# An expert layer in seven products a step: gathers asked tile by tile, weight sums spread over the step, another product order, a last step by tiles

## The chip, the cores and the metric

The kernel runs on one core of a Trainium2 chip. The metric is device time of one execution in microseconds, the median of several runs; lower is better. Beside the timed runs there is one profiled execution, whose trace all views here come from.

## The reference

The input x has shape (4, 8, 768, 32). A state-space block (Mamba-2 in chunks) makes y of the same shape; y is laid out as 3072 tokens of 256 numbers, and each token goes through the one expert that its id names:

```python
expert_idx = token_ids * np.int64(2654435761) % np.int64(E)      # E = 8
for e in range(E):
    mask = expert_idx == e
    xe = x[mask]                        # tokens of expert e, D = 256
    h = np.maximum(xe @ w1[e], 0.0)     # F = 1024
    out[mask] = h @ w2[e]
```

All is float32.

## The kernel before

**Two parts.** The first part (to about 85 us) computes the state-space block, stores the tokens' rows to a buffer in HBM (`y_tokens`), and works out from the ids a slot for every token. The change doesn't touch it, but for one constant of the slots. The second part runs the experts.

**Slots and tiles.** The experts are sorted by their number of tokens. Place p has two halves (j = 0, 1) of `HALF[p]` slots each, 202 down to 184; `base[p, j]` is where a half begins among 25 tiles of 128 slots. A tile k is fetched with `gather(k)` (line 477: an indirect DMA on POOL's queue, into one of 8 buffers `xg`), turned with `turn_x(k)` (line 485: two transposes on TensorE into PSUM bank `BT`, one copy by ACT into `xT`), and, when both products of all its slots are done, written out with `put(k, bank)` (line 836: two transposes into bank `BQ`, a copy by ACT into one of 4 buffers `o_sb`, and an indirect DMA on POOL's queue that scatters its rows). `ask(n)` issues the next n gathers.

**Seven products.** Each of an expert's two matrix products is cut into 2 x 2 blocks and done with seven block products instead of eight, after sums of the operands' blocks and before sums of the results, in Winograd's order of sums. `up(p, q0, what, bank, st)` (line 750) does product `what` (1 to 7) of the first matrix product for half of the rows (q0 = 0 or 2): two matmuls, and what DVE or ACT then does with the PSUM bank. `down` (line 801) does a product of the second, in four matmuls. The operands' sums are DVE's: `sums_x` (four sums over an expert's tokens), `sums_h` (four over its hidden tile, one in each of the slots 0 to 3), `sums_w1` and `sums_w2` (four each over an expert's weights, 128 x 512 elements).

Products 6, 7 and 4 of one half share a PSUM bank and add up in it; so do 5 and 3. After 6, DVE evicts `u2` = bank + p1; after 7, `u3` = bank + p1 (line 789); and 7's block also takes z, the bank of product 5, as `hx` = z + u3 (line 791), which ACT then puts through a ReLU. Product 4 may enter the bank only when `u3` has been read out, product 3 only when z has. In `down` it is the same with one bank each (lines 822 to 834).

**The order.** A manual schedule is on: the instructions of an engine run in the order in which the code writes them, and an engine waits at the one whose operands or buffers aren't ready, with all that stands behind it. `step(p)` writes the up products of expert p among the down products of expert p - 1, in seven slots. A slot holds up to two up products, one turn, one put and one down product. In slot 0 the four w1 sums for expert p + 1 follow, in slot 1 the four w2 sums for expert p; from slot 2 on, each slot asks for one gather; slot 4 has `sums_x(p + 1)`. At the end of a step the weights are loaded: two halves of w1 for p + 3, w2 for p + 1, on SyncE's queue. For p = 1, 2 the up products 1 and 2 have been done ahead (`UP_E` has five products), from p = 3 on all seven are in the step (`UP`). `step(E)` has the last expert's down products alone, and the last four puts follow it, then a loop for tokens beyond the slots, which has no rounds with this input.

## Time and profile before

| | |
|---|---|
| runs | 284.52, 287.68, 287.95 us; median 287.68 |
| profiled execution | 285.23 us, its span in the trace 283.4 us |
| busy share of the span | PE 79%, PEld 73%, DVE 71%, ACT 27%, POOL 28% |
| mean granted clock of TensorE | 0.92 |
| indirect DMAs | 25 gathers and 25 scatters, POOL's queue |
| from HBM, to HBM | 26.47 MB, 6.42 MB |

PE stands for TensorE's matmuls and PEld for its weight loads, which overlap them; each matmul in float32 appears as two instructions of the trace. A share over the whole span mixes the two parts, so the expert part is better read in stretches of time, one for each step: its rows give the busy time of each engine there. A row of the timeline has its start and length, and in brackets the idle time of its engine ahead of it, with what ended that.

### The profile page before, as it was taken

The page shows a single profiled execution, that of the slowest core. Times are in us where ns is not written, and L with a number is a line of the kernel's source. Part 1 is how long each engine was busy: PE and PEld are TensorE (multiplying, and loading weights), DVE is VectorE, ACT ScalarE, POOL GpSimd, SP SyncE. Part 2 cuts the span into 40 slices and gives each one's busy share as a digit, 9 for nine tenths or more (in the row PEclk, how much of TensorE's full clock was granted, in tenths as well). Part 3 has the DMA queues.
Part 4 walks back from the last instruction along what each step waited for, and adds up shares of the span by engine and source line. Part 5 has one row for each costly group of instructions (what it writes and reads, how often), then busy time and mean ns, then how long its engine had stood idle before and what let it go on. Part 6 is the DMA issues. An engine that isn't in the chain of part 4 may idle for free. (4 is left out here: it accounts for less than half of the span.)

```text
span 283.4 us, 6377 instructions
## 1 busy us (share of the span) xinstructions
PE 224.9 (79%) x2577; PEld 205.7 (73%) x2579; DVE 201.5 (71%) x393; ACT 76.3 (27%) x177; POOL 79.0 (28%) x113
## 2 busy tenths in 40 slices
PE   7885775576579768798799989499989999999820
PEld 2773654465469758788689989399979999998810
DVE  7879768999808529977977958836876886776310
ACT  4314152043116512210312223221242242313010
POOL 8800003019443760001121501710132130312250
PEclk9689799579958997999999999989999999999995
DMA  5899998507958334015316305610901500500110
GB/s 127 135 173 141 173 178 176 192 22 207 294 173 245 97 106 148 19 21 191 123 57 208 126 2 185 203 38 5 312 20 58 166 26 13 172 33 6 51 59 1
DMA packets 51890, 33.19 MB, mean 117 GB/s; under 512 B 30714, under 2 KB 46194, under 8 KB 51860
## 3 DMA queue, kind: packets, MB, share of 16 engines
q1 hardware_dynamic: 47444, 24.41, 34.4%
q0 software_dynamic: 2400, 6.43, 7.0%
q10 hardware_dynamic: 2016, 1.93, 2.3%
q8 instruction: 21, 0.34, 0.6%
q14 instruction: 9, 0.07, 0.1%
HBM read 26.47 MB, written 6.42 MB: 116 GB/s over the span
## 5 line engine op out<-in xcount | busy, mean ns | idle before, releaser
L847 POOL DMA_INDIRECT out_dram<-o_sb,idx_out x25 | 27.9, 1117 | 73.7 <-ACT o_sb L843 58.9
L480 POOL DMA_INDIRECT xg<-y_tokens,idx_in x25 | 27.5, 1098 | 75.3 <-PE ps L838 46.6
L770 PE MATMUL ps<-t,s 128*128 128x202 f32 (+7 forms) x192 | 37.6, 333 | 2.2 <-DVE t L730 1.6
L770 PEld LDWEIGHTS ps<-t,s 128*128 128x128 f32 x192 | 32.8, 194 | 3.2 <-ACT xT L494 1.8
L812 PE MATMUL ps<-t,s 128*128 128x202 f32 (+7 forms) x192 | 34.9, 326 | 0.0
L812 PEld LDWEIGHTS ps<-t,s 128*128 128x128 f32 x192 | 31.3, 190 | 0.0
L770 PE MATMUL ps<-xT,w 128*128 128x202 f32 (+7 forms) x128 | 26.2, 342 | 0.0
L792 ACT ACTIVATE hx<-hx 128x404 f32<-128x404 f32 (+7 forms) x16 | 8.4, 525 | 57.6 <-DVE hx L791 57.6
L770 PEld LDWEIGHTS ps<-xT,w 128*128 128x128 f32 x128 | 22.6, 200 | 0.8 <-ACT p1e L777 0.7
L572 PE MATMUL ps<-x,w 128*64 128x64 f32 x384 | 15.6, 251 | 7.1 <-issue 2.6
L572 PEld LDWEIGHTS ps<-x,w 128*64 128x64 f32 x384 | 14.7, 164 | 8.3 <-issue 4.5
L770 PE MATMUL ps<-t,w 128*128 128x202 f32 (+7 forms) x64 | 14.5, 351 | 7.1 <-DVE u L789 5.6
L528 DVE COPY_PREDICATED w<-cmask,ps 128x2048 f32<-128x2048 int32 x6 | 15.2, 2532 | 4.9 <-PE ps L523 4.9
L770 PEld LDWEIGHTS ps<-t,w 128*128 128x128 f32 x64 | 11.0, 198 | 9.1 <-DVE u L789 7.3
L838 PE MATMUL ps<-ident,xT 128*128 128x128 f32 x50 | 9.8, 281 | 6.7 <-ACT o_sb L843 6.1
L812 PE MATMUL ps<-hx,s 128*128 128x202 f32 (+7 forms) x64 | 12.1, 331 | 2.5 <-DVE xT L830 2.5
L770 PE MATMUL ps<-xT,s 128*128 128x202 f32 (+7 forms) x64 | 13.8, 344 | 0.0
L843 ACT ACTIVATE o_sb<-ps 128x256 f32<-128x256 f32 x23 | 8.7, 380 | 18.6 <-PE ps L838 12.2
L411 POOL TENSOR_SCALAR laneoh<-iota,lane 128x128 bf16<-128x128 f32 x12 | 9.0, 765 | 16.6 <-DVE stile L400 16.6
L494 ACT ACTIVATE xT<-ps 128x256 f32<-128x256 f32 x23 | 8.6, 377 | 16.6 <-PE ps L488 14.7
L523 PE MATMUL ps<-ce,bt 32*64 32x128 f32 x384 | 8.9, 315 | 5.1 <-ACT ce L251 2.8
L812 PEld LDWEIGHTS ps<-hx,s 128*128 128x128 f32 x64 | 10.5, 189 | 3.4 <-DVE xT L830 3.4
(189 smaller groups left out, 442.1 us busy)
## 6 DMA issues: line engine op xcount, KB each, us to landing
w<-in_moe_w_dram SPq DMA_DIRECT2D x8, 1024.0 KB, 6.4
w<-in_moe_w_dram SPq DMA_DIRECT2D x13, 512.0 KB, 4.8
x<-in_x_dram SPq DMA_DIRECT2D x12, 256.0 KB, 6.4
y_tokens<-y_sb SPq DMA_DIRECT2D x6, 512.0 KB, 3.4
w<-in_moe_w_dram ACTq DMA_DIRECT2D x3, 512.0 KB
raw<-in_B_dram SPq DMA_DIRECT2D x8, 128.0 KB, 6.0
raw<-in_C_dram SPq DMA_DIRECT2D x8, 128.0 KB, 4.7
raw<-in_B_dram SPq DMA_DIRECT2D x8, 64.0 KB, 2.1
```

The lines of the kernel that those rows point to most:

```text
L411: eng.tensor_scalar(out=laneoh[:, i], in0=iota_n, scalar1=lane[:, i:i + 1], scalar2=None, op0=OP.is_equal)
L480: pool_e.indirect_dma_start(out=xg[k], out_offset=None, in_=y_dram[0:n, :], in_offset=bass.IndirectOffsetOnAxis(ap=idx_in[:, k:k + 1], axi ...
L494: act.activation(o, i, AF.Copy)
L523: pe.matmul(out=ps[u * T:(u + 1) * T, BM + b, g * P:(g + 1) * P].rearrange("q (e i) -> q e i", e=2), lhsT=bts[k][r, g, c], rhs=ces[k][r, g ...
L528: dve.copy_predicated(out=m_sb, mask=cmask.bitcast(I32).rearrange("q j i -> q (j i)").unsqueeze(1).to_broadcast([P, NB, 2 * G * T]), data= ...
L572: pe.matmul(out=o[:, 0], lhsT=m_sb[:, b, h * T:(h + 1) * T], rhs=xs[k][:, b * H + h], start=first, stop=True, skip_group_check=True)
L770: pe.matmul(out=ps[:, bank, i * n:(i + 1) * n], lhsT=lhs[:, (q0 + i) * P:(q0 + i + 1) * P], rhs=rhs, start=(first and i == 0), stop=True, ...
L792: act.activation(hq(2), hq(2), AF.Relu)
L812: pe.matmul(out=ps[:, bank, 0:n], lhsT=lhs(q), rhs=rhs(q), start=(first and q == 0), stop=True, skip_group_check=True)
L838: pe.transpose(out=ps[:, bank, i * P:(i + 1) * P], in_=xT[:, i, k * P:(k + 1) * P], identity=ident)
L843: act.activation(o_sb, ps[:, bank, 0:DM], AF.Copy)
L847: st = pool_e.indirect_dma_start(out=out[:], out_offset=bass.IndirectOffsetOnAxis(ap=idx, axis=0), in_=o_sb, in_offset=None, bounds_check= ...
```

## The change

It has four parts.

1. *Gathers.* `ask(1)` moves from "each slot from 2 on" to right behind each `turn_x`. In POOL's queue, before (gathers write `xg`, scatters `out_dram`):

```order
L480 DMA xg<-y_tokens,idx_in 128x256 x23
L847 DMA out_dram<-o_sb,idx_out 3072x256
L480 DMA xg<-y_tokens,idx_in 128x256 x2
L847 DMA out_dram<-o_sb,idx_out 3072x256 x24
L953 TENSOR_LOAD nov_i
```

and now:

```order
L482 DMA xg<-y_tokens,idx_in 128x256 x19
L859 DMA out_dram<-o_sb,idx_out 3072x256
L482 DMA xg<-y_tokens,idx_in 128x256 x3
L859 DMA out_dram<-o_sb,idx_out 3072x256
L482 DMA xg<-y_tokens,idx_in 128x256
L859 DMA out_dram<-o_sb,idx_out 3072x256
L482 DMA xg<-y_tokens,idx_in 128x256
L859 DMA out_dram<-o_sb,idx_out 3072x256 x2
L482 DMA xg<-y_tokens,idx_in 128x256
L859 DMA out_dram<-o_sb,idx_out 3072x256 x20
L988 TENSOR_LOAD nov_i
```

The 25 gathers and 25 scatters stay; the last six gathers now stand among the scatters, each behind the turn of the tile whose buffer it takes, and 19 instead of 23 come ahead of the first scatter.

2. *Weight sums.* `sums_w1` and `sums_w2` become generators. Each slot takes one sum from each that has been started; w1's starts in slot 0 as before, w2's in slot 3 instead of 1.

3. *Order of products.* `down` has 1, 2, 6, 7, 5, 4, 3 instead of 1, 2, 6, 5, 7, 3, 4; in steps 1 and 2 the up products of both halves are interleaved (`UPS`), the second half's 6, 7 and 4 in bank 0. Whichever of 5 and 7 comes later makes `hx` = z + u3.

Parts 2 and 3 on DVE's queue at the start of step 1, before (`t` are the sums over the hidden tile and over tokens, `s` the weight sums, `u` and `hx` evictions of up products):

```order
L741 SCALAR_TENSOR_TENSOR t_1625<-hx,h_1496 128x808
L786 TENSOR_TENSOR u_1630<-ps,p1e 128x2x200
L711 TENSOR_TENSOR s_1643<-w_1224 128x512
L712 TENSOR_TENSOR s_1643<-s_1643,w_1224 128x512
L713 TENSOR_TENSOR s_1643<-w_1224 128x512
L714 TENSOR_TENSOR s_1643<-w_1224,s_1643 128x512
L744 TENSOR_TENSOR t_1625<-hx,t_1625 128x808
L789 TENSOR_TENSOR u_1651<-ps,p1e 128x2x200
L791 TENSOR_TENSOR hx<-ps,u_1651 128x2x200
```

and now:

```order
L741 SCALAR_TENSOR_TENSOR t_1621<-hx,h_1496 128x808
L786 TENSOR_TENSOR u_1626<-ps,p1e 128x2x200
L713 TENSOR_TENSOR s_1643<-w_1224 128x512
L744 TENSOR_TENSOR t_1621<-hx,t_1621 128x808
L789 TENSOR_TENSOR u_1648<-ps,p1e 128x2x200
L798 TENSOR_TENSOR hx<-ps,u_1648 128x2x200
L786 TENSOR_TENSOR u_1654<-ps,p1e 128x2x200
L713 TENSOR_TENSOR s_1643<-s_1643,w_1224 128x512
L746 SCALAR_TENSOR_TENSOR t_1621<-hx 128x808
L795 TENSOR_TENSOR hx<-ps,p1e 128x2x200
L793 TENSOR_TENSOR hx<-ps,u_1626 128x2x200
```

Between the first eviction `u` (product 6) and the second (product 7) stood four weight sums and one over the hidden tile; now there are one and one, and the four w2 sums that stood behind `hx` have gone from this place.

4. *The last step by tiles.* The last half of the last expert begins at a tile's start (48 slots ahead of it stay empty; there are 25 tiles as before). The step of the last down products is written out: order 1, 2, 6, 7, 4, 5, then the puts of the two tiles that need no product 3, then product 3 in two pieces of 128 and 56 columns, each with its eviction and its put, the copies by ACT and DVE in turn; a put now follows its slot's product. Behind the last put of the expert before, POOL gets a `drain()`, an instruction that waits until the engine has nothing left to do (the listing of the order leaves it out). TensorE's queue in the last step, before (`xT` are transposes for puts):

```order
L838 MATMUL ps<-ident,xT 128x128 x2
L812 MATMUL ps<-h_2525,w_2470 128x184 x4
L838 MATMUL ps<-ident,xT 128x128 x2
L812 MATMUL ps<-hx,w_2470 128x184 x4
L838 MATMUL ps<-ident,xT 128x128 x2
L812 MATMUL ps<-t_2595,s_2517 128x184 x12
L812 MATMUL ps<-hx,s_2517 128x184 x4
L812 MATMUL ps<-t_2595,w_2470 128x184 x4
L838 MATMUL ps<-ident,xT 128x128 x8
```

and now, from its second product on:

```order
L821 MATMUL ps<-hx,w_2470 128x184 x4
L850 MATMUL ps<-ident,xT 128x128 x2
L821 MATMUL ps<-t_2595,s_2553 128x184 x4
L850 MATMUL ps<-ident,xT 128x128 x2
L821 MATMUL ps<-t_2595,s_2553 128x184 x4
L821 MATMUL ps<-t_2595,w_2470 128x184 x4
L821 MATMUL ps<-t_2595,s_2553 128x184 x4
L850 MATMUL ps<-ident,xT 128x128 x4
L814 MATMUL ps<-hx,s_2553 128x128 x4
L850 MATMUL ps<-ident,xT 128x128 x2
L814 MATMUL ps<-hx,s_2553 128x56 x4
L850 MATMUL ps<-ident,xT 56x128 x2
```

All eight transposes stood behind the last product; now four stand ahead of product 3 and two behind each of its pieces.

The diff, cut to its core:

```diff
@@ slots
     for pj in order:
+        if pj == order[-1]:
+            at = -(-at // P) * P
         base[pj] = at
@@ weight sums
+    def sums_w(w, s, q):
+        q = [q(i // 2, i % 2) for i in range(4)]
+        for i, (x0, x1, op) in enumerate(((q[2], q[3], OP.add), (s[:, 0], q[0], OP.subtract),
+                                          (q[2], q[0], OP.subtract), (q[1], s[:, 1], OP.subtract))):
+            yield dve.tensor_tensor(out=s[:, i], in0=x0, in1=x1, op=op)
@@ up
         elif what == 7:
-            u3 = work("u3", 2)
-            dve.tensor_tensor(out=u3, in0=src, in1=st["p1"], op=OP.add)
-            z = ps[:, st["z"], 0:2 * n].rearrange("q (i n) -> q i n", i=2)
-            dve.tensor_tensor(out=hq(2), in0=z, in1=u3, op=OP.add)
-            act.activation(hq(2), hq(2), AF.Relu)
+            st["u3"] = work("u3", 2)
+            dve.tensor_tensor(out=st["u3"], in0=src, in1=st["p1"], op=OP.add)
...
+        if what in (5, 7) and "z" in st and "u3" in st:
+            dve.tensor_tensor(out=hq(2), in0=st["z"], in1=st["u3"], op=OP.add)
+            act.activation(hq(2), hq(2), AF.Relu)
@@ down
+        if parts:
+            for i, (c0, c1) in enumerate(parts):
+                for q in range(Q4):
+                    pe.matmul(out=ps[:, bank, c0:c1], lhsT=lhs(q), rhs=rhs(q)[:, c0:c1], start=False, stop=True,
+                              skip_group_check=True)
+                dve.tensor_tensor(out=xT[:, 0, slots(p, 1)][:, c0:c1], in0=ps[:, bank, c0:c1], in1=st["u2"][:, c0:c1],
+                                  op=OP.add)
+                put(slots(p, 1).start // P + i, (BQ, BT)[i], (act, dve)[i], c1 - c0)
+            return
@@ step
-    DOWN = [1, 2, 6, 5, 7, 3, 4]
+    UPS = [(0, 6, 1), (0, 5, 2), (0, 7, 1), (2, 6, 0), (0, 4, 1), (0, 3, 2), (2, 7, 0), (2, 5, 2), (2, 4, 0), (2, 3, 2)]
+    DOWN = [1, 2, 6, 7, 5, 4, 3]
...
                 turn_x(k)
                 turned.add(k)
+                ask(1)
...
             if s == 0 and 0 < p < E - 1:
-                sums_w1(p + 1, dve)
-            if s == 1 and 0 < p < E:
-                sums_w2(p, dve)
-            if s >= 2:
-                ask(1)
+                sums.append(sums_w1(p + 1))
+            if s == 3 and p > 0:
+                sums.append(sums_w2(p))
+            for x in sums:
+                next(x, None)
@@ the last step
-    for p in range(E + 1):
+    for p in range(E):
         step(p)
-    last = [k for k in outs if done_at[k] == E - 1]
-    for i, k in enumerate(last):
-        put(k, (BQ, BT, 0, 1)[i % 4], (act, dve)[i % 2])
+    dst = {}
+    puts = [k for k in outs if done_at[k] == E - 2]
+    for s, w in enumerate([1, 2, 6, 7, 4, 5]):
+        if s < 4:
+            sums_h(E - 1, s)
+        down(E - 1, w, 3 + BK[w], dst)
+        if puts:
+            put(puts.pop(0), BQ)
+            if not puts:
+                pool_e.drain()
...
+    mid = [k for k in outs if done_at[k] == E - 1 and k * P < base[E - 1, 1]]
+    for i, k in enumerate(mid):
+        put(k, (BQ, BT)[i % 2], (act, dve)[i % 2])
+    down(E - 1, 3, 3 + BK[3], dst, PARTS)
```

More of the change, by code (lines that the diff above doesn't have):

```diff
@@ L705, in slots, with sums_w1, sums_w2 @@
         return slice(base[p, j], base[p, j] + HALF[p])
-    def sums_w1(p, eng):
-        w = w1s[p]
-        q = lambda i, k: w[:, k, i * FH:(i + 1) * FH]
-        s = s1[p] = spool.tile([P, 4, FH], F32, name="s1")
-        eng.tensor_tensor(out=s[:, 0], in0=q(1, 0), in1=q(1, 1), op=OP.add)
-        eng.tensor_tensor(out=s[:, 1], in0=s[:, 0], in1=q(0, 0), op=OP.subtract)
-        eng.tensor_tensor(out=s[:, 2], in0=q(1, 0), in1=q(0, 0), op=OP.subtract)
-        eng.tensor_tensor(out=s[:, 3], in0=q(0, 1), in1=s[:, 1], op=OP.subtract)
-    def sums_w2(p, eng):
-        w = w2s[p]
-        q = lambda i, k: w[:, k * Q4:(k + 1) * Q4, i * P:(i + 1) * P]
-        s = s2[p] = spool.tile([P, 4, Q4, P], F32, name="s2")
-        eng.tensor_tensor(out=s[:, 0], in0=q(1, 0), in1=q(1, 1), op=OP.add)
-        eng.tensor_tensor(out=s[:, 1], in0=s[:, 0], in1=q(0, 0), op=OP.subtract)
-        eng.tensor_tensor(out=s[:, 2], in0=q(1, 0), in1=q(0, 0), op=OP.subtract)
-        eng.tensor_tensor(out=s[:, 3], in0=q(0, 1), in1=s[:, 1], op=OP.subtract)
+    def sums_w(w, s, q):
[3 more added lines that the diff above has]
+            yield dve.tensor_tensor(out=s[:, i], in0=x0, in1=x1, op=op)
+    def sums_w1(p):
+        w = w1s[p]
+        s1[p] = spool.tile([P, 4, FH], F32, name="s1")
+        return sums_w(w, s1[p], lambda i, k: w[:, k, i * FH:(i + 1) * FH])
+    def sums_w2(p):
+        w = w2s[p]
+        s2[p] = spool.tile([P, 4, Q4, P], F32, name="s2")
+        return sums_w(w, s2[p], lambda i, k: w[:, k * Q4:(k + 1) * Q4, i * P:(i + 1) * P])
     def sums_x(p):
@@ L799, in up, with down @@
             act.activation(hq(1), hq(1), AF.Relu)
-    def down(p, what, bank, st):
+        if what in (5, 7) and "z" in st and "u3" in st:
+            dve.tensor_tensor(out=hq(2), in0=st["z"], in1=st["u3"], op=OP.add)
+            act.activation(hq(2), hq(2), AF.Relu)
+    def down(p, what, bank, st, parts=()):
         n = HALF[p]
@@ L826, in down @@
             st["z"] = bank
+            if "u3" in st:
+                dve.tensor_tensor(out=o(1, 1), in0=src, in1=st["u3"], op=OP.add)
         elif what == 7:
-            u3 = work("du3")
+            u3 = st["u3"] = work("du3")
             dve.tensor_tensor(out=u3, in0=src, in1=st["p1"], op=OP.add)
-            dve.tensor_tensor(out=o(1, 1), in0=ps[:, st["z"], 0:n], in1=u3, op=OP.add)
+            if "z" in st:
+                dve.tensor_tensor(out=o(1, 1), in0=ps[:, st["z"], 0:n], in1=u3, op=OP.add)
         elif what == 3:
@@ L834, in down, with put @@
             dve.tensor_tensor(out=o(1, 0), in0=src, in1=st["p1"], op=OP.add)
-    def put(k, bank, eng=None):
+    def put(k, bank, eng=None, n=P):
         for i in range(DP):
-            pe.transpose(out=ps[:, bank, i * P:(i + 1) * P], in_=xT[:, i, k * P:(k + 1) * P], identity=ident)
+            pe.transpose(out=ps[0:n, bank, i * P:(i + 1) * P], in_=xT[:, i, k * P:k * P + n], identity=ident)
         o_sb = mwork.tile([P, DM], F32, name="o_sb", bufs=4)
         if eng is dve:
-            dve.tensor_copy(out=o_sb, in_=ps[:, bank, 0:DM])
+            dve.tensor_copy(out=o_sb[0:n], in_=ps[0:n, bank, 0:DM])
         else:
-            act.activation(o_sb, ps[:, bank, 0:DM], AF.Copy)
-        scatter(o_sb, idx_out[:, k:k + 1])
+            act.activation(o_sb[0:n], ps[0:n, bank, 0:DM], AF.Copy)
+        scatter(o_sb[0:n], idx_out[0:n, k:k + 1])
     def scatter(o_sb, idx):
@@ L880 @@
                 up(p, q0, what, (2 * p + 4 + q0 // 2) % 8, sts[p, q0])
-    sums_w1(1, dve)
-    sums_w2(0, dve)
+    list(sums_w1(1))
+    list(sums_w2(0))
     for i, k in enumerate(turn_due(0)):
@@ L890 @@
     UP_E = [6, 5, 7, 4, 3]
-    DOWN = [1, 2, 6, 5, 7, 3, 4]
+    UPS = [(0, 6, 1), (0, 5, 2), (0, 7, 1), (2, 6, 0), (0, 4, 1), (0, 3, 2), (2, 7, 0), (2, 5, 2), (2, 4, 0), (2, 3, 2)]
+    DOWN = [1, 2, 6, 7, 5, 4, 3]
     BK = {1: 0, 2: 0, 6: 1, 7: 1, 4: 1, 5: 2, 3: 2}
     outs = sorted(range(NK), key=lambda k: (done_at[k], k))
+    n1 = HALF[E - 1]
+    PARTS = [(c, min(c + P, n1)) for c in range(0, n1, P)]
+    assert base[E - 1, 1] % P == 0 and len(PARTS) == 2
     def step(p):
@@ L902, in step @@
             else:
-                ups = [(q0, w, BK[w]) for q0 in (0, 2) for w in (UP_E if p < NEAR - 1 else UP)]
+                ups = UPS if p < NEAR - 1 else [(q0, w, BK[w]) for q0 in (0, 2) for w in UP]
+        ups = list(ups)
+        sums = []
         downs = list(DOWN) if p > 0 else []
```

6 lines of the change are left out of this document (4 added, 2 removed).

## The prediction

> **What bounds the kernel now.** I first cut the expert part of the trace into its steps. Each row below is one stretch: start and end, its length, then the busy time of PE, PEld, DVE, ACT and POOL, the granted TensorE clock, and DMA. The first seven rows are steps 1 to 7, the eighth is the last step up to the end of the last scatter's issue, the ninth is what follows it.
>
> ```profile
> 110.13:131.42 21.29, 18.18 (x100) 17.22 (x100) 17.45 (x32) 3.50 (x8) 1.02 (x1) 0.96 0.29 96
> 131.42:152.18 20.76, 17.86 (x106) 16.86 (x106) 16.84 (x31) 4.12 (x10) 3.94 (x3) 1.00 0.37 119
> 152.18:173.51 21.33, 20.58 (x128) 19.77 (x127) 16.56 (x31) 6.43 (x17) 4.81 (x4) 1.00 0.26 82
> 173.51:198.85 25.34, 21.33 (x124) 20.75 (x124) 16.66 (x31) 5.95 (x15) 8.05 (x7) 0.93 0.36 118
> 198.85:220.47 21.62, 20.31 (x129) 19.45 (x129) 16.39 (x31) 6.74 (x18) 5.20 (x5) 1.00 0.36 125
> 220.47:239.98 19.51, 19.51 (x126) 18.91 (x125) 16.20 (x31) 5.94 (x16) 3.38 (x3) 1.00 0.24 75
> 239.98:258.36 18.38, 18.38 (x120) 18.14 (x119) 12.76 (x23) 5.15 (x13) 3.44 (x3) 1.00 0.24 80
> 258.36:276.38 18.02, 11.40 (x72) 10.05 (x69) 6.43 (x13) 2.45 (x7) 7.46 (x7) 0.98 0.13 45
> 276.38:283.40 7.02, 0.00 (x0) 0.00 (x0) 0.00 (x0) 0.00 (x0) 0.01 (x1) 0.50 0.01 1
> ```
>
> Steps 6 and 7 are TensorE without a hole. Step 4 does the same products as step 6 on a few more columns and is 5.8 us longer. Steps 1 and 2 have four products fewer and are still longer than step 6. So TensorE bounds the expert part wherever it isn't held up, and the change can win only its holes, plus the 25 us after 258.36. I then read the timeline of TensorE's weight loads and kept the rows with a wait (in brackets: idle time, and what ended it). Two grouped rows of the waits, for 152 to 258.3 us, stand for the small ones.
>
> ```profile
> 116.45 0.64 PEld L770 LDWEIGHTS ps<-t,w 128*128 128x128 f32 x4 [2.06 <-DVE u L789]
> 121.99 1.31 PEld L770 LDWEIGHTS ps<-t,s 128*128 128x128 f32 x8 [0.81 <-DVE hx L796]
> 128.57 1.33 PEld L812 LDWEIGHTS ps<-hx,s 128*128 128x128 f32 x8 [1.17 <-DVE xT L830]
> 137.33 0.63 PEld L770 LDWEIGHTS ps<-t,w 128*128 128x128 f32 x4 [2.25 <-DVE u L789]
> 142.85 1.30 PEld L770 LDWEIGHTS ps<-t,s 128*128 128x128 f32 x8 [0.40 <-DVE hx L796]
> 149.36 1.31 PEld L812 LDWEIGHTS ps<-hx,s 128*128 128x128 f32 x8 [1.17 <-DVE xT L830]
> 163.83 0.20 PEld L838 LDWEIGHTS ps<-ident,xT 128*128 128x128 f32 x2 [1.05 <-ACT o_sb L843]
> 182.21 0.20 PEld L838 LDWEIGHTS ps<-ident,xT 128*128 128x128 f32 x2 [4.25 <-ACT o_sb L843]
> 210.82 0.20 PEld L838 LDWEIGHTS ps<-ident,xT 128*128 128x128 f32 x2 [1.60 <-ACT o_sb L843]
> ...
> PEld ps L770 <- DVE u L789: 0.8, 4, 0.2
> PEld ps L488 <- ACT xT L494: 0.8, 3, 0.3
> ```
>
> The waits of steps 1 and 2 sum to 4.04 and 3.82 us; all six are for a DVE eviction that frees a PSUM bank.
>
> **Gathers behind the tile that frees their buffer.** What held TensorE at 182.21 is on the other queues (POOL, then ACT):
>
> ```profile
> 175.45 0.99 POOL L480 DMA_INDIRECT xg<-y_tokens,idx_in  x1 [13.82 <-PE ps L838]
> 176.75 1.09 POOL L847 DMA_INDIRECT out_dram<-o_sb,idx_out  x1 [0.30 <-issue]
> ...
> 181.78 0.38 ACT L843 ACTIVATE o_sb<-ps 128x256 f32<-128x256 f32 x1 [6.18 <-DMA out_dram<-o_sb,idx_out]
> ```
>
> The last gather stood 13.82 us at the head of POOL's queue, until the transposes of its buffer's tile; the scatters behind it started only then. With four output buffers the fifth copy of ACT waited for the scatter issued at 176.75, and TensorE for the copy. In the changed order a gather stands behind the turn that frees its buffer, so it waits for a transpose just done. The number of gathers and scatters stays. Each is still asked eight tiles, over two steps, ahead of its use. The hole cost more than its length:
>
> ```profile
> 184.26 1.47 PE L770 MATMUL ps<-xT,w 128*128 128x190 f32 x4
> 188.97 0.81 PE L770 MATMUL ps<-xT,w 128*128 128x190 f32 x4
> ...
> 182.20:186.80 4.60, 4.58 (x19) 4.48 (x20) 2.28 (x4) 1.96 (x6) 2.53 (x3) 0.63 0.24 85
> ```
>
> The same four instructions took 1.47 us at 184.26 and 0.81 at 188.97. With a granted clock of 0.63 over 4.60 us, 0.37 x 4.60 = 1.7 us went to slow clock. So step 4 loses 4.25 + 1.7. The Trainium skill (TensorE: Matmul & The Clock Gate, Part 1) says that an idle window of about 3.4 us halves the clock and as long a busy one restores it. The row agrees; by that rule, too, the slow stretch goes with its hole, and the sum stays.
>
> **Weight sums spread, products reordered.** The pitch on DVE comes from neighbours without idle time:
>
> ```profile
> 201.57 0.69 DVE L712 TENSOR_TENSOR s<-s,w 128x512 f32<-128x512 f32 x1
> 202.18 0.68 DVE L713 TENSOR_TENSOR s<-w 128x512 f32<-128x512 f32 x1
> ...
> 114.92 0.99 DVE L744 TENSOR_TENSOR t<-hx,t 128x808 f32<-128x808 f32 x1
> 115.83 0.57 DVE L789 TENSOR_TENSOR u<-ps,p1e 128x400 f32<-128x400 f32 x1
> ...
> 112.49 1.54 PE L812 MATMUL ps<-h,w 128*128 128x202 f32 x8
> 113.87 0.84 PE L770 MATMUL ps<-t,s 128*128 128x200 f32 x4
> ```
>
> A weight sum takes 0.61 us of the queue, a sum over the hidden tile 0.91, an eviction with its dependent one 0.6. A down product takes 1.38 us of TensorE, an up product about 0.68. In step 1 four weight sums (2.4 us) stood ahead of the eviction of product 7, and product 4 followed 7 at once in the same bank: 2.06. Now one sum stands ahead, and 0.68 + 1.38 = 2.06 us of other work lies between 7 and 4. For 121.99, the sums of w2 leave the place ahead of the eviction. For 128.57, product 3 of down no longer follows the read of its bank: product 4, 1.38 us, lies between, against one eviction (0.37) and some 0.27 for a product's end to reach DVE (1.54 less 1.38, the rest of it an estimate). Without waits step 1 is five slots of 2 x 0.68 + 1.38 and two of 1.38, 16.5 us, with 0.04 x 21.29 of slow clock 17.3 (that clock comes from step 0, which is left as it was). I walked both queues through these slots with the pitches: the bank is read 1.2 us before product 4 of the first half needs it, 1.1 before 5 of the second, 0.7 before 3 of down, and with nothing to spare before 4 of the second half. The limit is then close on both sides: DVE is busy 17.45 and 16.84 us there. So all 7.86 us is the upper bound; if DVE keeps half of its present idle time of 7.76 us, the gain is 3.9. I take **7.0**, nearer the walk.
>
> In steps 3 and 5 the waits 1.05 and 1.60 come from the same queue: ACT does its copies in order, behind a ReLU of a tile that DVE evicts after the lump of w2 sums. In step 5 that lump also waits for its load; it now starts two slots later. I take both as gone, and of the grouped rows 0.4 in step 3, 0.45 in 5, 0.5 in 6, 0.2 in 7 and 0.2 in 4.
>
> But a new wait comes. In slot 4 a w2 sum and the four sums over the next tokens stand ahead of the eviction of product 7 (second half), which product 4 needs:
>
> ```profile
> 215.76 0.36 DVE L830 TENSOR_TENSOR xT<-ps,du 128x190 f32<-128x190 f32 x1
> 216.03 0.34 DVE L729 TENSOR_TENSOR t<-xT 128x186 f32<-128x186 f32 x1
> 217.21 0.54 DVE L789 TENSOR_TENSOR u<-ps,p 128x376 f32<-128x376 f32 x1
> ```
>
> The four cost 217.21 - 216.03 = 1.18. One eviction (0.36), the weight sum (0.61), these four and the eviction itself (0.54), with 0.27 to reach DVE, make 2.96 against about 2.55 of TensorE work in between (two up products and a down product of these widths): **0.45** of stall (small signal times rounded in), in steps 3 to 6. Before, it was 0.2. If DVE is late besides, each 0.1 is paid four times.
>
> Steps, then: 7.0 (1 and 2); 1.45 - 0.45 = 1.0 (3); 4.25 + 0.2 + 1.7 - 0.45 = 5.7 (4); 2.05 - 0.45 = 1.6 (5); 0.05 (6); 0.2 (7). Sum **15.5**. Bounds: 3.9 + 4.25, about 8, if all else goes to the new wait; 18, if nothing does.
>
> **Last step by tiles.** The rows that carry it:
>
> ```profile
> 262.54 3.90 PE L812 MATMUL ps<-t,s 128*128 128x184 f32 x24
> 267.26 1.23 PEld L812 LDWEIGHTS ps<-hx,s 128*128 128x128 f32 x8 [1.10 <-DVE xT L830]
> 275.40 0.98 POOL L847 DMA_INDIRECT out_dram<-o_sb,idx_out  x1 [0.30 <-issue]
> ...
> L1030 POOLq DRAIN  x3: 45/103/4155, 278.4 to 283.2; - x3
> ```
>
> Now the last scatter starts 17.04 us after 258.36. In the new order, counted from the same place: three puts and products 1, 2, 6 until 4.9; product 7 to 6.6, 4 after the eviction of 7 to 8.6, 5 to 9.9; tiles 21 and 22 transposed by 10.3, their scatters from 10.9; product 3 in 128 and 56 columns to 11.4 and 13.1; scatters of tiles 23 and 24 from 13.4 and 14.7, at POOL's pitch of 0.98 + 0.30. That is 17.0 - 14.7 = 2.3, bounds 0 (the drain below holds POOL 2 us more) and 3 (no wait at 7 and 4); I take **2.1**. The last half's shift to a tile's start only changes constants: 25 tiles as before.
>
> The end drain of POOL takes 4155 ns once every scatter has landed; the two drains right behind it take 103 and 45. The added drain is issued after the 46th of 50 indirect DMAs, at about 6.8. Should the cost be upkeep per DMA, 4 of 50 are left, 0.33; should it be fixed, 4.16 stays. Bounds 0.05 and 4.16; I take 0.4, because the drains with nothing behind them are short, so a gain of **3.7**. If the added drain itself takes 4.2, it ends at 11.0, where the first of the scatters behind it is ready; if 2 us longer, the end is 2 us later. The Trainium skill (VectorE: DVE Perf Modes, The DRAIN you can't avoid) has such boilerplate drains at about 12 ns on all engines. The 4155 ns differ from that; by its rule the added drain would change nothing, which leaves the 3.7 out: the first rival below.
>
> **The sum.** 15.5 + 2.1 + 3.7 = 21.3 us, from 283.4 to 262.1 of span, 263.9 as a profiled execution (285.23 - 283.4 = 1.8 around it). The median of the three runs, 287.68, lies 2.45 above that execution; nothing here says which a new median is nearer, so I add most of it: **266** us.
>
> **The rivals.** *The drain costs the same at the end.* For it: 4155 ns with all DMAs landed. Against it: 103 and 45 just behind. It gives 266 + 3.7, about 270.
>
> *DVE becomes the bound in steps 1 and 2, and its lag is paid at the token sums after.* For it: 17.45 us of DVE work against 17.3 of the walk, and the place with nothing to spare. Against it: the walk has DVE waiting 1.5 us in step 1. The steps then win 8 instead of 15.5: 273 or 274.
>
> *Slower: the DVE queue falls behind for good.* Each slot now has a weight sum ahead of the next evictions, and a slot's eviction of product 7 has about 1.6 us to spare in steps 3 to 6 where no token sums stand. Should DVE fall further back than that, 0.6 us is bared in seven slots of seven steps, 29 us, more than the 21.3 won: 295. It decides from a lag of 1.6 us on. Against it: in steps 3 to 6 DVE works 16.2 to 16.7 us of 19.5 or more.
>
> *The change doesn't do what it says*: gathers still block POOL, since a turn itself comes late. Then steps 1, 2 and the end win, step 4 nothing: 272, within the range.
>
> **How the numbers follow.** Forecast 266: 0.54, its own range 262 to 269. Drain unchanged: 0.16. DVE bound: 0.18, gathers still blocking: 0.04. Queue behind for good, or something like it: 0.04. Some mixture that ends within 2% (282 to 293, about what a measurement of this kernel can tell from no change): 0.04. Faster by over 2% 0.92, within 0.04, slower 0.04. The range, 261 to 276, takes in the cases of 270 to 274 and the bounds of the drain.
>
> **What would show it.** Right: no weight load waits over 1 us in steps 1 to 5; TensorE's clock 1.00 in step 4; no gather with a long wait ahead of a scatter; steps 1 and 2 at 17 to 18 us; the end drain well below 1 us, and a long one around 250. Wrong: DVE without idle time in steps 1 and 2 while TensorE waits for `u`, waits for product 4 over 1 us in steps 3 to 6, or a POOL drain that holds the last four scatters.

## The result, and the profile after

The changed kernel takes **261.36 us** (median of 4 executions, 259.69 to 264.52) against 286.10 (median of 4, 282.06 to 287.95): a ratio of **0.9197**, 95% interval 0.9114 to 0.9281. On another chip, with 5 rounds, it was 263.68 against 285.74, ratio 0.9191 (0.9145 to 0.9237). The ratios leave disturbed executions out, the medians don't (one of the experiments below has 309.87 us among its four). The profiled execution took 259.69 us, its span 258.0.

The same stretches as before the change, steps 1 to 7 in the first seven rows, the last step up to the end of the last scatter's issue in the eighth, the rest in the ninth (start and end, length, busy PE, PEld, DVE, ACT, POOL, granted TensorE clock, DMA):

```profile
105.16:122.21 17.05, 17.02 (x98) 16.53 (x99) 16.26 (x32) 4.22 (x9) 1.00 (x1) 1.00 0.40 130
122.21:139.35 17.14, 17.14 (x105) 16.89 (x105) 16.04 (x32) 3.99 (x10) 4.95 (x4) 1.00 0.49 153
139.35:159.72 20.37, 20.29 (x128) 19.90 (x127) 16.74 (x32) 6.42 (x17) 8.52 (x7) 1.00 0.34 103
159.72:179.30 19.58, 19.47 (x123) 19.12 (x123) 16.11 (x31) 5.87 (x15) 3.57 (x3) 1.00 0.38 127
179.30:199.37 20.07, 19.95 (x130) 19.56 (x129) 16.02 (x31) 6.77 (x18) 5.24 (x5) 1.00 0.45 150
199.37:218.83 19.46, 19.33 (x127) 18.99 (x126) 15.92 (x31) 6.07 (x16) 3.27 (x3) 1.00 0.25 77
218.83:237.03 18.20, 18.20 (x119) 18.16 (x119) 12.39 (x23) 5.26 (x13) 2.95 (x3) 1.00 0.18 61
237.03:253.49 16.46, 12.35 (x80) 10.73 (x78) 7.19 (x15) 2.40 (x7) 7.54 (x7) 0.95 0.13 45
253.49:258.00 4.51, 0.00 (x0) 0.00 (x0) 0.00 (x0) 0.00 (x0) 0.00 (x0) 0.50 0.06 18
```

TensorE now has work in all but 0.13 us or less of each of steps 1 to 7 (compare length and first number), at a granted clock of 1.00. Step 4 fell from 25.34 to 19.58. Of TensorE's weight loads in steps 2 to 7, these alone wait over 0.3 us:

```profile
156.97 0.62 PEld L770 LDWEIGHTS ps<-t,w 128*128 128x128 f32 x4 [0.38 <-DVE u L789]
176.61 0.62 PEld L770 LDWEIGHTS ps<-t,w 128*128 128x128 f32 x4 [0.41 <-DVE u L789]
196.71 0.62 PEld L770 LDWEIGHTS ps<-t,w 128*128 128x128 f32 x4 [0.41 <-DVE u L789]
216.19 0.61 PEld L770 LDWEIGHTS ps<-t,w 128*128 128x128 f32 x4 [0.42 <-DVE u L789]
```

That is the new wait forecast for product 4 of the second half, one in each of steps 3 to 6. On POOL's queue a gather and the scatter behind it in step 4, the scatter ahead of the added drain, and the four last ones:

```profile
161.66 1.05 POOL L482 DMA_INDIRECT xg<-y_tokens,idx_in  x1 [9.53 <-PE ps L850]
163.01 1.54 POOL L859 DMA_INDIRECT out_dram<-o_sb,idx_out  x1 [0.31 <-issue]
...
242.80 1.18 POOL L859 DMA_INDIRECT out_dram<-o_sb,idx_out  x1 [0.49 <-ACT o_sb L855]
248.69 0.98 POOL L859 DMA_INDIRECT out_dram<-o_sb,idx_out  x1 [4.70 <-ACT o_sb L855]
249.97 0.98 POOL L859 DMA_INDIRECT out_dram<-o_sb,idx_out  x1 [0.30 <-issue]
251.26 0.98 POOL L859 DMA_INDIRECT out_dram<-o_sb,idx_out  x1 [0.30 <-issue]
252.55 0.94 POOL L859 DMA_INDIRECT out_dram<-o_sb,idx_out  x1 [0.31 <-DVEq L993]
```

Then POOL's drains, the added one and those at the end (min, median and max ns; first and last start):

```profile
L980 POOLq DRAIN  x1: 5257/5257/5257, 242.6 to 242.6; - x1
...
L1065 POOLq DRAIN  x3: 46/103/387, 256.8 to 257.7; - x3
```

The end drain fell from 4155 to 387 ns; the added one lasts from 242.6 to 247.8.

The spans differ by 25.4 us. To say where, I cut every trace at the first product of each step; the last step runs from its first down product to the start of the last scatter, the tail from there to the end. Lengths in us, here and for the experiments told below:

| kernel | ahead | 0 | 1 | 2 | 3 | 4 | 5 | 6 | 7 | last | tail |
|---|---|---|---|---|---|---|---|---|---|---|---|
| before | 97.98 | 12.15 | 21.28 | 20.76 | 21.33 | 25.34 | 21.62 | 19.51 | 19.16 | 16.26 | 8.03 |
| changed | 96.97 | 8.20 | 17.05 | 17.14 | 20.36 | 19.59 | 20.07 | 19.45 | 18.21 | 15.52 | 5.44 |
| b_gather | 98.18 | 13.25 | 22.20 | 20.75 | 21.33 | 19.75 | 21.60 | 19.51 | 19.16 | 16.27 | 8.03 |
| b_sums | 99.32 | 11.82 | 18.72 | 19.19 | 20.76 | 25.43 | 20.46 | 19.84 | 18.98 | 16.27 | 8.03 |
| b_order | 99.55 | 13.31 | 19.46 | 18.91 | 21.65 | 24.85 | 21.34 | 19.62 | 18.53 | 15.75 | 8.02 |
| b_last | 97.08 | 13.53 | 22.15 | 20.76 | 21.33 | 26.25 | 21.93 | 19.50 | 18.24 | 15.51 | 5.11 |
| a_nodrain | 100.96 | 8.19 | 17.05 | 17.14 | 20.36 | 19.58 | 20.07 | 19.45 | 18.21 | 14.88 | 9.03 |
| a_gather | 102.97 | 8.19 | 17.05 | 17.14 | 20.36 | 23.21 | 20.07 | 19.45 | 18.21 | 15.52 | 5.28 |
| a_sums | 101.50 | 8.19 | 20.01 | 18.91 | 21.19 | 20.32 | 21.23 | 19.62 | 18.31 | 15.88 | 5.25 |
| a_order | 95.15 | 8.20 | 19.23 | 19.20 | 20.76 | 19.97 | 20.46 | 19.84 | 18.21 | 15.51 | 5.27 |
| same_before | 99.21 | 13.64 | 22.19 | 20.76 | 21.34 | 26.50 | 22.13 | 19.51 | 19.08 | 16.27 | 8.03 |
| same_after | 98.35 | 13.36 | 16.81 | 17.14 | 20.36 | 19.58 | 20.07 | 19.45 | 18.21 | 15.53 | 4.58 |
| a_best | 98.04 | 9.24 | 17.10 | 17.15 | 20.02 | 19.21 | 19.68 | 19.05 | 18.21 | 14.88 | 5.14 |

Of the 25.4 us, 20.5 lie from step 1 on, where the prediction put 21.3; 4.97 lie ahead of step 1, 3.95 of them in step 0, which the prediction left as it was. Of the 20.5, some 0.8 belong to step 0 as well: before, its slow clock reached 1.6 us into step 1 (0.96 there), and after the short step 0 it doesn't (1.00).

### The profile page after: what moved, and what is told of

It is laid out like the page before. It is cut to its first block, busy times and chain, and to the rows that moved or that the text cites. A ratio compares the mean times of both kernels' runs of the same rounds, so it can differ in the third digit from the quotient of the medians.

```text
span 258.0 us, 6404 instructions
## 1 busy us (share of the span) xinstructions
PE 222.2 (86%) x2587; PEld 204.7 (79%) x2587; DVE 198.1 (77%) x394; ACT 76.3 (30%) x177; POOL 78.9 (31%) x113
## 4 chain that ended last, share of the span: by engine, by line
PE 49%; DVE 18%; DMA 15%; issue 4%; SPq 4%; POOL 3%; ACT 3%; ACTq 0%; DVEq 0%; POOLq 0%
PE ps L770 25%; PE ps L821 20%; DMA out_dram<-o_sb,idx_out 10%; POOL laneoh L413 3%; DVE w L530 3%; SPq L126 2%; DMA xg<-y_tokens,idx_in 2%; DVE rows L236 2%; DVE ct L243 2%; PE ps L490 2%; DVE bt L243 2%; DVE u L789 1%; PE ps L850 1%; DMA raw<-in_C_dram 1%; ACT ce L253 1%
## 5 line engine op out<-in xcount | busy, mean ns | idle before, releaser
L859 POOL DMA_INDIRECT out_dram<-o_sb,idx_out x25 | 28.5, 1138 | 71.3 <-ACT o_sb L855 57.1
L482 POOL DMA_INDIRECT xg<-y_tokens,idx_in x25 | 26.8, 1071 | 54.6 <-PE ps L850 35.2
L770 PE MATMUL ps<-t,s 128*128 128x202 f32 (+7 forms) x192 | 36.4, 327 | 1.6 <-DVE t L730 1.6
L821 PE MATMUL ps<-t,s 128*128 128x202 f32 (+7 forms) x192 | 35.3, 326 | 0.3 <-DVE du L833 0.3
L770 PEld LDWEIGHTS ps<-t,s 128*128 128x128 f32 x192 | 31.8, 189 | 2.5 <-ACT xT L496 1.8
L821 PEld LDWEIGHTS ps<-t,s 128*128 128x128 f32 x192 | 31.4, 189 | 0.5 <-DVE du L833 0.5
L799 ACT ACTIVATE hx<-hx 128x404 f32<-128x404 f32 (+7 forms) x16 | 8.4, 525 | 52.3 <-DVE hx L798 52.3
L713 DVE TENSOR_TENSOR s<-w 128x512 f32<-128x512 f32 x32 | 21.8, 682 | 0.0
L770 PE MATMUL ps<-t,w 128*128 128x202 f32 (+7 forms) x64 | 13.8, 338 | 0.6
L525 PE MATMUL ps<-ce,bt 32*64 32x128 f32 x384 | 10.0, 346 | 4.8 <-ACT ce L253 2.8
L770 PE MATMUL ps<-xT,s 128*128 128x202 f32 (+7 forms) x64 | 12.9, 326 | 0.0
L525 PEld LDWEIGHTS ps<-ce,bt 32*64 32x64 f32 x384 | 8.0, 171 | 5.6 <-ACT ce L253 3.2
L796 ACT ACTIVATE hx<-hx 128x404 f32<-128x404 f32 (+7 forms) x16 | 8.3, 525 | 13.1 <-DVE hx L795 13.1
L821 PE MATMUL ps<-t,w 128*128 128x202 f32 (+7 forms) x64 | 11.8, 327 | 0.4 <-DVE du L840 0.4
```

Source lines behind the costliest of these rows:

```text
L482: pool_e.indirect_dma_start(out=xg[k], out_offset=None, in_=y_dram[0:n, :], in_offset=bass.IndirectOffsetOnAxis(ap=idx_in[:, k:k + 1], axi ...
L525: pe.matmul(out=ps[u * T:(u + 1) * T, BM + b, g * P:(g + 1) * P].rearrange("q (e i) -> q e i", e=2), lhsT=bts[k][r, g, c], rhs=ces[k][r, g ...
L713: yield dve.tensor_tensor(out=s[:, i], in0=x0, in1=x1, op=op)
L770: pe.matmul(out=ps[:, bank, i * n:(i + 1) * n], lhsT=lhs[:, (q0 + i) * P:(q0 + i + 1) * P], rhs=rhs, start=(first and i == 0), stop=True, ...
L799: act.activation(hq(2), hq(2), AF.Relu)
L821: pe.matmul(out=ps[:, bank, 0:n], lhsT=lhs(q), rhs=rhs(q), start=(first and q == 0), stop=True, skip_group_check=True)
```

## Experiments

**One part alone, on the kernel before.** Four kernels, on one chip. The gathers:

```diff
                 turned.add(k)
+                ask(1)
...
-            if s >= 2:
-                ask(1)
```

> Kernel before with one part alone: a gather asked right behind each turn instead of one in every slot from the third on. My theory: the hole of step 4 (4.25 us) and its slow clock (1.7) go, and with them the small waits of TensorE for ACT's copies in steps 3 and 5 stay, since these come from the w2 sums: 5.5 to 6.5 us less, ratio about 0.979. The stretch before step 1 stays as it was (step 0 about 12.2 us with its clock of 0.5 at the end). Rival: the 4 us that step 0 lost in the changed kernel come from the gathers' new places, too: step 0 at 8.2 us here and about 10 us less in all, ratio 0.965. Second rival: the gain shows only together with the new order, and this alone wins 4.25 or less.

280.45 us against 285.98, ratio 0.9825 (0.9719 to 0.9931). Steps 3 and 4 of this kernel:

```profile
154.38:175.71 21.33, 20.59 (x128) 19.77 (x128) 16.56 (x31) 6.42 (x17) 8.12 (x7) 1.00 0.31 98
175.71:195.46 19.75, 19.75 (x124) 19.04 (x123) 16.48 (x31) 5.74 (x15) 3.17 (x3) 1.00 0.39 127
```

Step 4 lost its hole and its slow clock, 5.59 us; step 3 is unmoved, as said. The gathers' part stands by itself. Step 0 is 13.25, so the gathers' places did not shorten it.

The weight sums:

```diff
-                sums_w1(p + 1, dve)
-            if s == 1 and 0 < p < E:
-                sums_w2(p, dve)
+                sums.append(sums_w1(p + 1))
+            if s == 3 and 0 < p < E:
+                sums.append(sums_w2(p))
+            for x in sums:
+                next(x, None)
```

> Kernel before with one part alone: the weight sums spread, one of each list in a slot (w1 from the first slot, w2 from the fourth), with the old order of products and the old gathers. My theory: of the waits in steps 1 and 2 the ones before product 4 (2.06, 2.25) shrink but stay, since 4 still follows 7 at once (about 1.0 each: the pitch of one weight sum 0.6 plus the evictions), the ones before 5 of the second half (0.81, 0.40) go, the ones of 1.17 before 3 of down stay: 2 to 4 us less, ratio about 0.99. Rival: the lumps of sums alone made all six waits, and the whole 7 us of steps 1 and 2 come with this part: ratio 0.975.

279.79 us, ratio 0.9818 (0.9737 to 0.9899). The waits over 0.5 us left in steps 1 and 2:

```profile
115.59 0.64 PEld L768 LDWEIGHTS ps<-t,w 128*128 128x128 f32 x4 [0.98 <-DVE u L787]
127.01 1.33 PEld L810 LDWEIGHTS ps<-hx,s 128*128 128x128 f32 x8 [1.18 <-DVE xT L828]
134.48 0.63 PEld L768 LDWEIGHTS ps<-t,w 128*128 128x128 f32 x4 [0.97 <-DVE u L787]
146.24 1.31 PEld L810 LDWEIGHTS ps<-hx,s 128*128 128x128 f32 x8 [1.17 <-DVE xT L828]
```

The waits before product 4 fell from 2.06 and 2.25 to about 1.0, those before 5 went, those before product 3 of down stayed. Steps 1 and 2 won 4.1 us, steps 3 and 5 another 1.7, from the lump of w2 sums that had held ACT's copies; from step 1 on it is 5.6, more than the 2 to 4 I had expected, which left steps 3 and 5 out. The rival, all of the 7 us of steps 1 and 2 by this part, fell by these waits; the interval of the ratio alone would not exclude it.

The order of products:

```diff
-    DOWN = [1, 2, 6, 5, 7, 3, 4]
+    UPS = [(0, 6, 1), (0, 5, 2), (0, 7, 1), (2, 6, 0), (0, 4, 1), (0, 3, 2), (2, 7, 0), (2, 5, 2), (2, 4, 0), (2, 3, 2)]
+    DOWN = [1, 2, 6, 7, 5, 4, 3]
```

> Kernel before with one part alone: the new order of the products of up in steps 1 and 2 and of down everywhere, with the weight sums in lumps of four and the old gathers. My theory: the wait of 1.17 before product 3 of down goes (2.3 us in two steps), the one before 4 of the first half shrinks by what now lies between (2.06), so that 0 to 0.5 of it is left, but a lump of four sums (2.4 us) still stands ahead of an eviction and bares up to 1 us a lump: 3 to 5 us less, ratio about 0.985. Rival: with the lumps left the new order wins nothing, since DVE is late by the lump wherever it stands: 0.995 or above.

279.81 us, ratio 0.9796 (0.9698 to 0.9895). The waits over 0.5 us in steps 1 and 2:

```profile
119.20 0.64 PEld L770 LDWEIGHTS ps<-t,w 128*128 128x128 f32 x4 [0.59 <-DVE u L789]
124.70 0.64 PEld L770 LDWEIGHTS ps<-t,s 128*128 128x128 f32 x4 [2.14 <-DVE hx L793]
143.70 0.63 PEld L770 LDWEIGHTS ps<-t,s 128*128 128x128 f32 x4 [1.80 <-DVE hx L793]
```

Product 3 of down waits no more, and product 4 waits 0.59 once; but the lumps of w1 and w2 sums, which follow each other in the first two slots, now bare 2.14 and 1.80 before product 5 of the second half, twice what I had expected of a lump. Steps 1 and 2 still won 3.7 us, so the rival (nothing without the spread) fell too.

The last step:

```diff
+        if pj == order[-1]:
+            at = -(-at // P) * P
...
-    for p in range(E + 1):
+    for p in range(E):
         step(p)
...
+            if not puts:
+                pool_e.drain()
...
+    down(E - 1, 3, 3 + BK[3], dst, PARTS)
```

> Kernel before with one part alone: the last step by tiles, with the last half's slots moved to a tile's start and the added drain of POOL after the 46th of its 50 indirect DMAs. Steps 0 to 7 are as before. My theory: the last step 1.5 to 2.1 us shorter up to the last scatter, the end drain 0.39 instead of 4.16 us, 1.2 us of this given back in what POOL does between the last scatter and the drain: 4 to 4.5 us less, ratio about 0.985, and steps 0 to 7 within 1 us of before, step 0 at about 12 us. Rival: the part wins 6 us, since what the tail gives back in the changed kernel has to do with the other parts.

281.88 us, ratio 0.9884 (0.9798 to 0.9969). Step 7 and the last step together won 1.67, the tail 2.92: 4.6 us by the trace, where the time shows 3.3; step 4 was 0.9 longer here than before, with its clock at 0.5 for 6.8 us instead of 3.4. By the ratios alone each part is only known to win between 0.3% and 3%; the sizes come from the stages. By stages the four parts win 5.6, 5.6, 5.2 and 4.6 us from step 1 on (step 1 left out for the first and steps 1, 4 and 5 for the last, where nothing was edited and the clock differs): 21.0, against 20.5 of the whole change. They add up to within 0.5 us. The experiments below price two of the parts otherwise, though (3.5 for the gathers, 7.9 for the sums): what a part is worth depends on what stands beside it.

**One part undone, on the changed kernel.** Four kernels, on a second chip, where the kernel before took 283.68 us. Here the table is compared from the start of step 0, since the stretch ahead varies from 95 to 103 us with the same instructions in it.

Without the added drain:

```diff
-            if not puts:
-                pool_e.drain()
```

> Changed kernel without the added drain of POOL; all else as changed. My theory: the drain costs by the indirect DMAs since the last one, some 83 ns each, so the end drain is back at 4.16 us (now 0.39); the four last scatters start up to 0.9 us earlier, since nothing holds POOL ahead of them, and the landing of the last scatter, 3.3 us after its start in the changed kernel against 2.1 in the kernel before, is short again (the 1.2 us given back belong to the drain): 1.7 to 2.9 us slower than the changed kernel, about 264 us. Rival: the landing stays at 3.3 us, since it belongs to the scatter of 56 rows and not to the drain: then 2.9 to 3.8 slower, about 265.

266.92 us, ratio to the kernel before 0.9433 (0.9365 to 0.9501); 2.94 us longer by the trace. The first of the four last scatters and the end drains:

```profile
252.01 0.98 POOL L859 DMA_INDIRECT out_dram<-o_sb,idx_out  x1 [4.05 <-ACT o_sb L855]
```

```profile
L1063 POOLq DRAIN  x3: 40/103/4163, 259.9 to 264.7; - x3
```

The first scatter starts 11.00 us after the last step's start (252.01 less 241.01) against 11.66 with the drain, so the drain holds it by 0.66, and the last scatter by 0.64; the end drain is back at 4163 ns. The stretch from the last scatter to the end drain stayed as long (4.0 us; 4.2 in the changed kernel, 3.0 before): my theory that the drain causes this fell, and the rival's 2.9 came. All kernels with the old last step have 3.0 and all with the new one 3.4 to 4.2, b_last among them, so it comes with the last step. The DMA packets between the end of the last scatter's issue and the end drain, first in the kernel before (276.3 to 278.4 us), then in the changed one (253.4 to 256.7), give a likely reason:

```profile
DMA packets 48, 0.01 MB, mean 4 GB/s; under 512 B 46, under 2 KB 46, under 8 KB 48
```

```profile
DMA packets 36, 0.08 MB, mean 25 GB/s; under 512 B 19, under 2 KB 19, under 8 KB 35
q8 instruction: 1, 0.02, 1.8%
```

Before, two packets of more than 512 B were left to move there, now 16, since the last tile now holds 56 rows of tokens. And one packet of 16 KB, on a queue that the profile calls instruction, now falls among them. Before, it ended 1.8 us ahead of the last scatter; in the changed kernel it ends 2.00 us after that scatter's start, and in the same kernel on the third chip 1.14. Between these two traces the tail differs by as much, 0.86 us (5.44 and 4.58). I did not try a kernel with the shift of the slots alone, nor one that moves this packet.

The old places of the gathers:

```diff
-                ask(1)
...
+            if s >= 2:
+                ask(1)
```

> Changed kernel with the old places of the gathers alone: one asked in every slot from the third on. My theory: a gather is again at POOL's head for over 9 us in steps 3 and 4, ACT's copies wait for the scatters behind it, and the hole in step 4 (4 to 5 us) with its slow clock (1.7) is back, somewhat smaller since the steps are shorter: 4 to 6 us slower, about 266 to 267 us, in steps 3 and 4 alone, and step 0 as in the changed kernel (8.2 us). Rival: the old places are what made step 0 long (11.8 to 13.5 us in the kernel before and the four with one part alone), and here it is 12 us again: 8 to 10 us slower.

267.19 us, ratio 0.9332 (0.9213 to 0.9451); 3.46 us longer by the trace, all of it in step 4 (3.62, less 0.16 in the tail). The hole, then step 4's row:

```profile
173.76 0.20 PEld L850 LDWEIGHTS ps<-ident,xT 128*128 128x128 f32 x2 [3.59 <-ACT o_sb L855]
```

```profile
165.72:188.92 23.20, 19.73 (x123) 19.12 (x123) 16.11 (x31) 5.95 (x15) 8.08 (x7) 1.00 0.39 131
```

The hole is back, at 3.59, but not the slow clock (1.00): 0.5 under my lower bound. Step 0 stays at 8.19, so its length again has nothing to do with the gathers.

The weight sums in lumps:

```diff
-                sums.append(sums_w1(p + 1))
-            if s == 3 and p > 0:
-                sums.append(sums_w2(p))
-            for x in sums:
-                next(x, None)
+                list(sums_w1(p + 1))
+            if s == 1 and p > 0:
+                list(sums_w2(p))
```

> Changed kernel with the weight sums in lumps of four (w1 in the first slot, w2 in the second), all else as changed. My theory, from the kernel with the new order alone, whose steps 1 and 2 took 19.5 and 18.9 us against 17.05 and 17.14 of the changed kernel: 4.2 us more in steps 1 and 2, 0 to 2 in steps 3 to 6, where the new wait of 0.4 a step goes with the w2 sum that stands ahead of the token sums: 3 to 6 us slower, about 266. Rival: spreading matters in steps 1 and 2 only because the steps before them ended late, and the loss here is under 2 us.

271.43 us (266.43 to 272.11; before 283.68); 7.9 us longer by the trace, more than I had expected. Three waits (4.9) stand against the 4.7 us that steps 1 and 2 lost:

```profile
116.59 0.64 PEld L770 LDWEIGHTS ps<-t,w 128*128 128x128 f32 x4 [0.98 <-DVE u L789]
122.08 0.64 PEld L770 LDWEIGHTS ps<-t,s 128*128 128x128 f32 x4 [2.13 <-DVE hx L793]
141.08 0.63 PEld L770 LDWEIGHTS ps<-t,s 128*128 128x128 f32 x4 [1.80 <-DVE hx L793]
```

Steps 3 to 6 lost 2.9, although their four waits of 0.4 went: TensorE again waits there for ACT's copies (1.04 at 160.26, 1.38 at 201.88) and for a DVE eviction (0.97 at 180.95).

The old order of products:

```diff
-    DOWN = [1, 2, 6, 7, 5, 4, 3]
+    DOWN = [1, 2, 6, 5, 7, 3, 4]
...
-                ups = UPS if p < NEAR - 1 else [(q0, w, BK[w]) for q0 in (0, 2) for w in UP]
+                ups = [(q0, w, BK[w]) for q0 in (0, 2) for w in (UP_E if p < NEAR - 1 else UP)]
```

> Changed kernel with the old order of products in steps 1 to 7 (up by halves, down with 5 ahead of 7 and 3 ahead of 4), all else as changed; the last step keeps its own order. My theory, from the kernel with spread sums alone, whose steps 1 and 2 took 18.7 and 19.2: 3.7 us more in steps 1 and 2, 1 to 2 in steps 3 to 7 where product 3 of down waits again for the read of its bank: 4 to 6 us slower, about 266. Rival: the order tells only beside lumps of sums, and with spread sums the loss is under 2 us. Step 0, which neither order touches, tells whether its length (8.2 us in the changed kernel's trace, about 12 in the others) varies by execution.

265.94 us (263.59 to 270.88; before 283.68); 5.6 us longer by the trace, 4.2 of it in steps 1 and 2. The waits over 0.5 us of step 1 are nearly those of the kernel with spread sums alone:

```profile
108.31 0.64 PEld L770 LDWEIGHTS ps<-t,w 128*128 128x128 f32 x4 [1.09 <-DVE u L789]
119.73 1.33 PEld L821 LDWEIGHTS ps<-hx,s 128*128 128x128 f32 x8 [1.18 <-DVE xT L842]
```

So spread and order are two remedies for two kinds of wait: sums ahead of an eviction, and a product straight behind the eviction of its own bank. Neither does the other's work.

**Both kernels on one chip, and a further version.** Two kernels are unchanged; the third adds to the changed one:

```diff
                 put(puts.pop(0), BQ)
+                if p == E - 1 and not puts:
+                    pool_e.drain()
...
-                if p + 1 < E:
-                    sums_x(p + 1)
+            if p + 1 < E and s == nslot - (3 if p < NEAR - 1 else 2):
+                sums_x(p + 1)
```

> The kernel before, unchanged, for its trace on the same chip as the next two. Up to the first products of step 1 its instructions and waits are those of the changed kernel, yet all five traces made from the kernel before (it and four with one part alone, these four on one chip) show step 0 at 11.8 to 13.5 us, and all five made from the changed kernel (it and four with one part undone, these four on another chip) 8.2. My theory: step 0's length belongs to the chip, not to the change: here 8.2 us, if the changed kernel beside it has 8.2 (or about 12 in both). Rival: it belongs to the program behind: here about 12 us, in the changed kernel beside it 8.2.

> The changed kernel, unchanged, on the same chip as the other two. From the start of step 0 on I expect the lengths of its first trace to 0.1 us each in steps 1 to 7 (17.05, 17.14, 20.36, 19.6, 20.1, 19.45, 18.2), the last step 15.5 and the tail 5.3 to 5.4, since the traces of the variants repeat these wherever the program is the same; what varies by execution lies before step 0. About 261 to 264 us. Rival: the steps vary as much as the whole does (2 to 4 us).

> Changed kernel with two additions: one more drain of POOL in step 7, behind that step's last scatter, and in steps 3 to 6 the four token sums one slot later, behind the eviction of product 7 of the second half instead of ahead of it. My theory: the wait of 0.4 us before product 4 goes in each of steps 3 to 6 (1.6 us), the drain in step 7 takes about 3.6 us (43 indirect DMAs by 84 ns) while POOL has nothing else to do, the one in the last step 0.3 instead of 3.9 us, so that the last scatters start 0.64 us earlier, as without any drain, and the end drain stays at 0.39: 2.3 us faster than the changed kernel, ratio to it about 0.991. Rivals: a drain costs 4 to 5 us wherever it stands, then the last step is no shorter; the token sums one slot later make the next step's first products wait, then steps 4 to 7 win less than 0.4 each or lose.

Step 0 of the kernel before, then of the changed kernel, on this chip:

```profile
99.21:112.84 13.63, 10.32 (x44) 9.93 (x45) 6.53 (x15) 2.87 (x6) 5.03 (x6) 0.76 0.27 79
```

```profile
98.35:111.71 13.36, 10.69 (x44) 9.77 (x45) 6.63 (x15) 2.88 (x6) 5.45 (x6) 0.76 0.29 85
```

Both are long. So the 3.95 us that step 0 won in the first pair of traces are no fixed part of the change. Whether the change makes a short step 0 likelier stays open: of seven traces with the changed kernel or a variant of it, five have 8.2, but none of the six with the kernel before or one part alone has under 11.8. The third kernel, with the same step 0 and on the same chip, had 9.24: it is no fixed property of a chip either. From step 1 on the changed kernel repeats its first trace to 0.02 us a step, apart from step 1 itself (16.81, 0.24 less) and the tail; what varies by execution lies in the part ahead, step 0 and step 1's start.

The third kernel: 262.33 us, ratio to the kernel before 0.9192 (0.9147 to 0.9238), beside 263.68 and 0.9191 for the changed one: the time does not tell them apart. The trace does. Its drains in step 7, in the last step and at the end:

```profile
L943 POOLq DRAIN  x1: 4810/4810/4810, 227.8 to 227.8; - x1
...
L982 POOLq DRAIN  x1: 3019/3019/3019, 243.2 to 243.2; - x1
...
L1067 POOLq DRAIN  x3: 46/103/377, 256.5 to 257.4; - x3
```

and its steps 3 to 6:

```profile
141.52:161.54 20.02, 20.02 (x128) 19.93 (x128) 16.19 (x31) 5.90 (x16) 8.52 (x7) 1.00 0.34 106
161.54:180.75 19.21, 19.21 (x124) 19.15 (x124) 16.09 (x32) 5.87 (x15) 3.94 (x3) 1.00 0.39 131
180.75:200.42 19.67, 19.67 (x129) 19.58 (x129) 16.00 (x32) 6.77 (x18) 4.91 (x5) 1.00 0.45 147
200.42:219.48 19.06, 19.06 (x127) 19.01 (x126) 15.92 (x32) 6.07 (x16) 2.95 (x3) 1.00 0.24 77
```

TensorE has no hole left there (1.5 us less over the four steps), and the last step is 14.88, as without any drain, with the end drain still at 377 ns: 2.2 us of the 2.3 expected. Against the variation ahead of step 1 a difference of this size needs more executions than 6.

## Why the prediction was right, step by step

Terms against the traces of the first pair (span 283.4 to 258.0):

| term | said | measured |
|---|---|---|
| steps 1 and 2 | 7.0 | 7.85, with 0.8 of clock |
| step 3 | 1.0 | 0.97 |
| step 4 | 5.7 | 5.75 |
| step 5 | 1.6 | 1.55 |
| step 6 | 0.05 | 0.06 |
| step 7 and last step | 0.2 + 2.1 | 1.7 |
| end drain, tail | 3.7 | 2.6 |
| sum | 21.3 | 20.5 |
| ahead of step 1 | 0 | 4.97 |

*Steps 1 and 2.* All six waits went, and the queue keeps up although it is busy 16.26 of 17.05 us: the rival "DVE becomes the bound" fell. That 7.85 is nearly the 7.86 that the waits summed to is luck. The prediction kept 0.04 x 21.29 = 0.85 us of slow clock in step 1, and this went too, with the short step 0. Without it the steps won the 7.0 of the forecast. The 0.86 held back for a late DVE was needed: 0.65 of it stands in two waits for DVE at the start of step 1 (0.32 at 105.16, 0.33 at 106.13).

*Steps 3 to 6.* Right to 0.1 us each, the new wait of 0.45 (measured 0.38 to 0.42) among them. Its cause is shown by a_best: with the token sums behind the eviction it is gone.

*Step 4.* The mechanism, a gather at POOL's head that holds scatters and through them ACT's copies, is shown from both sides (b_gather, a_gather). The sign I had named for it was badly put: a gather with 9.53 us of idle time ahead of a scatter is still there (161.66). POOL merely had nothing ready then: ACT makes no copy between 150.48 and 161.70, the scatter behind follows in 0.31, and no copy of ACT waits for a DMA.

*Last step.* Too large by 0.6: the added drain holds the scatters by 0.64 (a_nodrain), which I had only as a bound of 2. So one sign that I had named for being wrong, a drain that holds the last four scatters, did come, at a third of that size.

*The drain.* Right in kind: upkeep per DMA, not a fixed cost, so the rival at 270 fell. The drain itself won 3.77. The tail won 1.2 less, since the end drain starts that much later behind the last scatter (4.2 us against 3.0). I had written that the shift of the slots only changes constants; it puts 56 rows of tokens into the last tile. Some 0.9 of the 1.2 goes with the instruction packet, whose place varies by execution.

*The slow clock* is the term that I had fixed too tightly. I counted one slow stretch for step 4, which the first pair has, and said that the one at step 1's start would stay, which it did not. On the third chip the kernel before had a clock of 0.91 in step 1 and 0.87 in step 4:

```profile
112.84:135.04 22.20, 19.01 (x100) 18.35 (x100) 17.34 (x31) 3.22 (x7) 1.00 (x1) 0.91 0.25 89
...
177.14:203.64 26.50, 22.47 (x124) 21.91 (x124) 16.66 (x31) 5.98 (x15) 8.10 (x7) 0.87 0.34 112
```

0.13 of 26.5 is 3.4 us in step 4, twice my 1.7, and 0.09 of 22.2 is 2.0 in step 1. The changed kernel, after a step 0 as slow, had 0.99 in step 1: it lacks the wait of 2.64 us that brought a second slow stretch there. From step 1 on this pair differs by 24.1 us (175.8 to 151.7). The ratio of times says 23.1 us (21.8 to 24.4), a little more than 21.3.

*The median.* 261.36 lies 4.6 under the forecast of 266, just below that forecast's own range (262 to 269) and at the edge of the whole range (261 to 276). By the traces, 4.97 came from ahead of step 1, where the pair on the third chip differs by 1.1 only. With that stretch as before the span would have been 263.0, and with step 1's slow clock 263.8, against the 262.1 forecast. So the terms together were some 1.7 us too large, and luck ahead of step 1 more than made up for it.
